# LN3's bias on GpSimd, the query transposes on TensorE: one change with three parts

## The chip, the cores and the metric

The kernel runs on one core of a Trainium2 chip. The metric is device time in microseconds (us) of one execution. TensorE (PE) multiplies matrices, VectorE (DVE), ScalarE (ACT) and GpSimd (POOL) work on vectors, and SyncE (SP) issues most DMAs. DMAs are also issued from ScalarE's and GpSimd's instruction streams, and stand in order with their other instructions.

## The reference

The input x has 2048 rows of 1024 bf16 values. What is computed:

```
h  = x + A(layernorm(x))                 # LN1, sliding dilated attention
out = h + B(layernorm(h))                # LN2, gated MLP that mixes over rows

A: q, k, v = x @ wqkv   (32 heads of 32); each row attends to 8 rows: itself and 2, 4, .. 14 back;
   softmax over these 8; @ wo
B: z = gelu(x @ w_in)   (2048 x 3584); z1 = first 1792 columns;
   z2 = layernorm(last 1792 columns)     # LN3
   g = w_sp @ z2 + b_sp[:, None]         # w_sp is 2048 x 2048
   (z1 * g) @ w_out
layernorm(x) = (x - mean) / sqrt(var + 1e-5), without weights
```

## The kernel before, in words

**Tiling.** Rows are worked on in 16 tiles of 128 (NT) and 4 chunks of 512 (NCH), with 4 tiles to a chunk (TPC). Weights sit in SBUF as bf16. A TensorE accumulator `acc` is 128 x 1024 fp32 in PSUM. Three of them turn round (`ps_acc`, bufs=3), and the tiles `tpa` into which TensorE transposes share this ring.

**Stage 1: the queries of chunk 0, in an order written out by hand.** For each tile of chunk 0, `ln(i)` takes statistics (lines 243 to 245), gets the reciprocal deviation (249, 250) and writes the normalised tile `xn` (255). The projection needs it transposed, in `xnT[0]`, eight blocks of 128 x 128 for a tile. `xpose` (line 267) transposes blocks on TensorE against the identity and lets ScalarE copy them out of PSUM (269), in two copies of four blocks each. `XPE` says how many of a tile's blocks go this way: 8, 8, 6 and 4. The other blocks, the last two of tile 2 and the last four of tile 3, are transposed by a DMA that is issued from ScalarE's queue (line 314). The loop over i runs the 16 matmuls of tile i (line 305). In their midst, after `XAT[i]` matmuls, stands the transposition of tile i+1. Then come `ln(i + 2)`, the copy of the queries to `qs0` on ScalarE (311), the DMA transpose of tile i+2's remaining blocks, and on SP a DMA transpose of `qs0` into `qT` for the attention (315). The load of the value weights, wv (316), is bound to come behind the last of these on SP. The key weights, wk, are loaded by line 237.

**Stage 2: from the keys of chunk 0 to the end of the first half of B, ordered by a planner.** `Order` is a list scheduler that runs while the program is built. Operations are added with an engine, an estimated duration, what they depend on, a priority and a latency. It starts from estimated clocks (TensorE 22.3, ScalarE 23.4, VectorE and GpSimd 18.0), and emits the operations in the order of their planned start. TensorE, ScalarE and VectorE keep that order. SP's and GpSimd's own order is chosen by the compiler's scheduler. The planner holds the key, value and query projections (`qkv`, line 398), the attention (`attention`: VectorE products L454, sums L457, logits on TensorE L506, weighted sums L609 and L611), the output projection with LN2 (`head`, matmuls L666), and the two parts of z (`b_z2`, L736; `b_z1`, L786). Chunk by chunk, TensorE does projections while VectorE does the attention.

**LN3.** In `b_z2`, ScalarE empties the accumulators into `u` with the gelu and sums up (743), then sums the squares (752). `batch_rstd` makes mean, variance and the power -1/2 from these sums: four small VectorE instructions (630 to 633), the power on GpSimd (635), and on VectorE the bias `nb` = -mean x rstd (639). For chunks 0 to 2 ScalarE then normalises the four tiles of `u` in place (765) with scale rstd and bias nb, and each is stored to `z2_d` (769). A tile of `u` can be written for the next chunk when its store is done. For chunk 3 VectorE normalises into `z2sb` (767), with mean and rstd.

**x of the later chunks.** `x_loads` (called behind chunk 1's transposes in the program's order) loads x tiles 8 and 9 one by one (`load_x`, line 215), and 10 to 15 as three pairs (line 823). ScalarE reads them for LN1's sums (362).

**Stage 3: the mixing over rows and the output projection** (L897, L903, L919, L921), with all of `z2sb` in SBUF. Its order is written out by hand. The change doesn't touch it.

Of the kernel before, what the change touches and what calls it, by code (L numbers as in the profile page):

```python
# [12 lines left out]
ALU = mybir.AluOpType  # L13
# [6 lines left out]
F, FH = 3584, 1792  # L20
P = 128
NT = S // P
CH = 512
NCH = S // CH
TPC = CH // P
# [7 lines left out]
NWARM = 11  # L33
XRB = 4
XAT = (12, 13, 10, 0)
XPE = (8, 8, 6, 4)
POOLLAT = 2.2
LMODE = (2, 2, 2, 2)
Z2ACT = (4, 4, 4, 0)
FILL = (0, 2, 2, 0)  # L40
ABDMA = ((0, 1), (0, 1), (0, 1), (0, 1))
SPLIT = 4
# [97 lines left out]
def kernel(  # L140
# [121 lines left out]
    def xpose(i, xn, *parts):  # L262
        for k0, k1 in parts:
            if i not in tps or i == 0:
                tps[i] = (ps_acc if i or k0 else ps_att).tile([P, KT, P], BF16, name="tpa" if i or k0 else "tp0", tag="acc" if i or k0 else "L")
            for a in range(k0, k1):
                T.transpose(tps[i][:, a, :], xn[:, a * P:(a + 1) * P], ident)
        for k0, k1 in parts:
            A.copy(xnT[0][:, k0:k1, i * P:(i + 1) * P], tps[i][:, k0:k1, :])
# [16 lines left out]
    with tc.manual_schedule(engines=manual):  # L286
        wsq = l1.tile([P, 1], FP32, name="wsq", tag="wsq")
        A.activation(wsq[:], eps_t[:], ACTF.Sqrt)
        xns = {}

        def ln(i):
            stats(i)
            rstd_of(i)
            xns[i] = norm(i)

        ln(0)
        for part in ((0, 2), (2, 5), (5, KT)):
            xpose(0, xns[0], part)
        ln(1)
        for i in range(TPC):  # L300
            acc = new_acc()
            for n, (nh, kt) in enumerate([(nh, kt) for kt in range(KT) for nh in range(2)]):
                if n == XAT[i] and i + 1 < TPC:
                    xpose(i + 1, xns[i + 1], (0, 4), *([(4, XPE[i + 1])] if XPE[i + 1] > 4 else []))
                T.matmul(acc[:, nh, :], xnT[0][:, kt, i * P:(i + 1) * P], wsb[0][:, kt, nh * CH:(nh + 1) * CH],  # L305
                         start=(kt == 0), stop=(kt == KT - 1))
            if i + 2 < TPC:
                ln(i + 2)
            if i == 0:
                qs0 = att.tile([P, TPC, DLO, P], BF16, name="qs0", tag="oT")  # L310
            A.copy(qs0[:, i], acc[:].rearrange("p a b -> p (a b)").rearrange("p (m dl) -> p dl m", dl=DLO))
            if i + 2 < TPC:
                j, kd = i + 2, XPE[i + 2]
                A.dma_start_transpose(xnT[0][:, kd:KT, j * P:(j + 1) * P], xns[j][:, kd * P:])
            qt_ = nc.sync.dma_start_transpose(att_in[0][0][:, :, i * P:(i + 1) * P], qs0[:, i])
    tc.add_manual_dep(dma(wsb[2][:], wq_view[:, :, 2 * D:3 * D]).ins, qt_.ins.name,
                      mybir.DependencyInfo(mybir.DependencyClass.NoSync, mybir.DependencyReason.DATA), reason="load wv behind the query transposes")
# [304 lines left out]
                G["avmid", c] = m_  # L622
        G["avdone", c], G["avq", c] = m_, oq

    def batch_rstd(key, sums, sqs, n, pfx, deps, prio, cols=slice(0, TPC), nb=True):
        def a1():
            if cols.start == 0:
                G[key] = {k: bp.tile([P, TPC], FP32, name=pfx + k, tag=pfx + k) for k in ("mean", "msq", "var", "rstd", "nb")}
            t = G[key]
            V.tensor_scalar(t["mean"][:, cols], sums(), 1.0 / n, None, op0=ALU.mult)  # L630
            V.tensor_tensor(t["msq"][:, cols], t["mean"][:, cols], t["mean"][:, cols], op=ALU.mult)
            V.scalar_tensor_tensor(t["var"][:, cols], sqs(), 1.0 / n, t["msq"][:, cols], op0=ALU.mult, op1=ALU.subtract)
            V.tensor_scalar(t["var"][:, cols], t["var"][:, cols], 0.0, EPS, op0=ALU.max, op1=ALU.add)
        s1 = add("DVE", 0.74, a1, deps, prio=prio)
        s2 = add("POOL", 1.05, lambda: nc.gpsimd.tensor_tensor(G[key]["rstd"][:, cols], G[key]["var"][:, cols], nhalf[:, cols], op=ALU.pow),
                 [s1], lat=POOLLAT)
        def a3():
            t = G[key]
            V.scalar_tensor_tensor(t["nb"][:, cols], t["mean"][:, cols], -1.0, t["rstd"][:, cols], op0=ALU.mult, op1=ALU.mult)
        return add("DVE", 0.16, a3, [s2], prio=prio) if nb else s2  # L640

    def head(c):
# [74 lines left out]
    def b_z2(c):  # L717
        st = {}
        sqd = []
        for il in range(TPC):  # L720
            evs = []
            for hf in range(2):
                wd = win_specs[hf][1]
                deps = [G["hnTs", c][il] if ("hnTs", c) in G else G["hnT", c], G["win", hf]]
                for half in range(4):
                    def mm(half=half, hf=hf, il=il, wd=wd):
                        if half == 0:
                            st["acc"] = G["accz", c, il, hf] = new_acc()
                            if il == 0 and hf == 0:
                                st["sums"] = bp.tile([P, TPC, 2], FP32, name="sums", tag="sums")  # L730
                                st["sqs"] = bp.tile([P, TPC], FP32, name="sqs", tag="sqs")
                        accf = G["accz", c, il, hf][:].rearrange("p a b -> p (a b)")
                        for kt in range(2 * half, 2 * half + 2):
                            for n0 in range(0, wd, CH):
                                n1 = min(n0 + CH, wd)
                                T.matmul(accf[:, n0:n1], hnTs[c][:, il, kt, :], wins[hf][:, kt, n0:n1],  # L736
                                         start=(kt == 0), stop=(kt == KT - 1))
                    m_ = add("PE", 0.8635 if hf == 0 else 0.65, mm, deps, prio=order(), take="acc" if half == 0 else None)
                    deps = [(m_, 0.0)]
                def ev(hf=hf, il=il, wd=wd):  # L740
                    if hf == 0:
                        st["u", il] = l1.tile([P, FH], BF16, name="u", tag="x4k", bufs=4)
                    A.activation(st["u", il][:, hf * 1024:hf * 1024 + wd], G["accz", c, il, hf][:].rearrange("p a b -> p (a b)")[:, 0:wd],
                                 ACTF.Gelu_apprx_tanh, accum_out=st["sums"][:, il, hf:hf + 1])
                evs.append(add("ACT", 1.02 if hf == 0 else 0.93, ev, [m_] + ([G["z2st", c - 1, il]] if c else []),
                               prio=2.0, free="acc", lat=0.25, table="gelu"))
            def sq(il=il):
                if c < NCH - 1:
                    junk = pools["bq"].tile([P, FH], BF16, name="junk", tag="junk", bufs=1)[:]
                else:  # L750
                    junk = z2sb[c * TPC + il][:]
                A.activation(junk, st["u", il][:], ACTF.Square, accum_out=st["sqs"][:, il:il + 1])
            sqd.append(add("ACT", 1.72, sq, evs + ([G["close"]] if c == NCH - 1 else [G["open"]]), prio=5.0, lat=0.25))
        def st_tot():
            st["stot"] = bp.tile([P, TPC], FP32, name="stot", tag="stot")
            V.tensor_tensor(st["stot"][:], st["sums"][:, :, 0], st["sums"][:, :, 1], op=ALU.add)
        s0 = add("DVE", 0.16, st_tot, sqd, prio=2.0)
        rs = batch_rstd(("l3", c), lambda: st["stot"][:], lambda: st["sqs"][:], FH, "l3", [s0], 2.0)
        for il in range(TPC):
            i = c * TPC + il  # L760
            def nrm(il=il, i=i):
                t = G["l3", c]
                z2 = st["u", il] if c < NCH - 1 else z2sb[i]
                if Z2ACT[c] > il:
                    A.activation(z2[:], st["u", il][:], ACTF.Identity, scale=t["rstd"][:, il:il + 1], bias=t["nb"][:, il:il + 1])
                else:
                    V.tensor_scalar(z2[:], st["u", il][:], t["mean"][:, il:il + 1], t["rstd"][:, il:il + 1], op0=ALU.subtract, op1=ALU.mult)
                if c < NCH - 1:
                    dma(z2_d[i * P:(i + 1) * P, :], z2[:])
            n_ = add("ACT", 1.75, nrm, [rs], prio=5.5) if Z2ACT[c] > il else add("DVE", 0.62, nrm, [rs], prio=2.5)  # L770
            G["z2st", c, il] = dma_op(3.0, lambda: None, [n_])
            G["z2n", c, il] = n_

# [41 lines left out]

    dma_op(8.0, load_wo, [G["ev", 0, 2, 1]])
    def x_loads():
        for i in range(2 * TPC, 2 * TPC + 2):
            load_x(i)
        for i in range(2 * TPC + 2, NT, 2):  # L820
            x_slot(i)
            x_slot(i + 1)
            dma(pairs[i // 2][:], x2d[i * P:(i + 2) * P, :].rearrange("(a p) d -> p a d", p=P))

    for c in range(1, NCH):
        ln1(c)
# [123 lines left out]
```

## Time and profile before

| | |
|---|---|
| time, median of 13 runs | 725.81 us (724.85 to 730.58) |
| profiled execution | 725.17 us, span 723.4 us |
| granted TensorE clock | 1.0 |
| TensorE busy | 712.3 us (98% of the span) |
| VectorE, ScalarE, GpSimd busy | 412.5, 235.7, 59.1 us |
| first matmul of the key projection (L398) | 24.81 us |
| last key, value or query projection | up to 193 us |
| first matmul of the mixing (L897) | 430.15 us |

The span runs from the first to the last event of the core's engines. The time of an execution also holds what lies around it. Positions are us from the start of the span. In a line of the timeline stand start, length, engine, line of the kernel, operation, what is written from what, the count, and in brackets how long the engine was idle before and what ended it. A "q" behind an engine's name is its instruction queue, as at a DMA's issue. In a line of the chain stand start, length and what ran. PEld is TensorE's loading of weights, which runs beside its matmuls.

### The profile page before, as it was taken

Reading aid. Unit: us, or ns where it says so; the run is one execution under the profiler, and the core shown is the slowest. Engines: PE = TensorE matmul, PEld = TensorE weight load, DVE = VectorE, ACT = ScalarE, POOL = GpSimd, SP = SyncE. Lnnn points to the kernel's source line nnn. Section 1 sums busy time; section 2 is a strip of 40 time slices with the busy share of each in tenths; the row PEclk is TensorE's granted clock in tenths of the full one; section 3 lists DMA queues with packets and bytes.
Section 4 is the critical chain, followed back from the end, with each engine's and each line's share of the span. In section 5 each row is a group of like instructions: output and inputs, shape, how many; then the busy total and the mean of one; then the engine's idle time right before and its main releaser. Section 6 shows DMA issues by size and latency. Waiting matters only on the chain.

```text
span 723.4 us, 8399 instructions
## 1 busy us (share of the span) xinstructions
PE 712.3 (98%) x3382; PEld 363.5 (50%) x3443; DVE 412.5 (57%) x445; ACT 235.7 (33%) x300; POOL 59.1 (8%) x75
## 2 busy tenths in 40 slices
PE   8899999999999999999999999999999999999998
PEld 3566665666644444445444444444444444444444
DVE  5698699989999899987970202222222222222222
ACT  4389452632346685766725520000000000000000
POOL 0011400012002202001114000000000000000000
PEclk9999999999999999999999999999999999999999
DMA  9995674567662951752338878453115311120002
GB/s 329 237 319 128 197 195 147 160 201 253 215 253 80 236 194 56 258 126 59 136 114 263 258 188 291 161 131 123 37 43 134 119 39 44 33 85 14 1 16 72
DMA packets 120790, 107.55 MB, mean 149 GB/s; under 512 B 73696, under 2 KB 99072, under 8 KB 120752
## 3 DMA queue, kind: packets, MB, share of 16 engines
q1 hardware_dynamic: 110592, 73.95, 34.8%
q0 software_dynamic: 7888, 31.43, 13.0%
q10 hardware_dynamic: 2272, 1.64, 1.0%
q8 instruction: 27, 0.44, 0.3%
q14 instruction: 11, 0.09, 0.0%
HBM read 55.09 MB, written 30.74 MB: 119 GB/s over the span
## 4 chain that ended last, share of the span: by engine, by line
PE 96%; DMA 2%; issue 1%; DVE 0%; SPq 0%; ACT 0%; ACTq 0%
PE acc L897 27%; PE acc L398 21%; PE acc L786 13%; PE acc L736 13%; PE acc L919 13%; PE acc L666 8%; DMA xp<-in_A_x_dram 1%; DMA xnT<-xn 1%; PE acc L305 1%; PE L L506 1%; SPq L233 0%; DVE bnst L243 0%; DVE bnst L244 0%; DVE xn L255 0%; DVE ot L921 0%
## 5 line engine op out<-in xcount | busy, mean ns | idle before, releaser
L897 PE MATMUL acc<-wspT,z2sb 128*128 128x512 bf16 x878 | 193.1, 379 | 0.9
L897 PEld LDWEIGHTS <-z2sb 128*128 128x128 bf16 x896 | 87.7, 98 | 105.7
L903 DVE TENSOR_TENSOR g<-acc,bB 128x1024 bf16<-128x1024 f32 x28 | 34.3, 1225 | 159.9 <-PE acc L897 135.1
L786 PE MATMUL acc<-hnT,win 128*128 128x512 bf16 x448 | 98.0, 379 | 0.0
L736 PE MATMUL acc<-win,hnT 128*128 128x512 bf16 (+1 forms) x501 | 97.3, 352 | 0.6
L736 PEld LDWEIGHTS <-hnT 128*128 128x128 bf16 x512 | 50.0, 98 | 47.3 <-issue 0.4
L919 PEld LDWEIGHTS <-zg 128*128 128x128 bf16 x462 | 45.2, 98 | 51.7
L786 PEld LDWEIGHTS <-win 128*128 128x128 bf16 x448 | 43.8, 98 | 52.6 <-issue 0.4
L454 DVE TENSOR_TENSOR prod<-qT,kT 128x4096 bf16<-128x4096 bf16 (+1 forms) x32 | 68.3, 2152 | 2.2 <-DMA kT<-qkv_d 1.6
L609 DVE TENSOR_TENSOR prod<-vT,AB 128x4096 bf16<-128x4096 bf16 (+1 forms) x32 | 64.3, 2023 | 0.7
L611 DVE TENSOR_TENSOR oT<-oT,prod 128x4096 bf16<-128x4096 bf16 (+1 forms) x32 | 64.5, 2018 | 0.1
L921 DVE TENSOR_TENSOR ot<-acc,hr 128x1024 bf16<-128x1024 f32 (+2 forms) x18 | 19.9, 1106 | 73.1 <-PE acc L919 64.2
L919 PE MATMUL acc<-wout_a,zg 128*128 128x512 bf16 (+1 forms) x260 | 58.0, 372 | 0.3
L398 PE MATMUL acc<-xnT,wk 128*128 128x512 bf16 x249 | 55.7, 379 | 0.5 <-issue 0.2
L666 PE MATMUL acc<-wo_sb,oT 128*128 128x512 bf16 x249 | 55.7, 379 | 0.4
L398 PE MATMUL acc<-xnT,wv 128*128 128x512 bf16 x252 | 55.7, 379 | 0.2
L409 ACT CAST stg<-acc 128x1024 bf16<-128x1024 f32 x36 | 36.4, 1010 | 57.3 <-PE acc L398 53.5
L398 PEld LDWEIGHTS <-wk 128*128 128x128 bf16 x256 | 36.9, 145 | 18.7 <-issue 0.4
L398 PEld LDWEIGHTS <-wv 128*128 128x128 bf16 x256 | 37.0, 145 | 18.2
L919 PE MATMUL acc<-wout_b,zg 128*128 128x512 bf16 (+1 forms) x193 | 43.8, 372 | 0.2
L398 PE MATMUL acc<-xnT,wq 128*128 128x512 bf16 x189 | 41.8, 379 | 0.3 <-issue 0.2
L792 ACT ACTIVATE z1s<-acc 128x1024 bf16<-128x1024 f32 x28 | 28.6, 1022 | 40.7 <-PE acc L786 30.6
(102 smaller groups left out, 507.0 us busy)
## 6 DMA issues: line engine op xcount, KB each, us to landing
qkv_d<-stg SPq DMA_DIRECT2D x36, 256.0 KB, 2.5
z_d<-z1s SPq DMA_DIRECT2D x28, 256.0 KB, 2.7
z1c<-z_d SPq DMA_DIRECT2D x28, 256.0 KB, 3.2
z_d<-u SPq DMA_DIRECT2D x12, 448.0 KB, 2.5
z2sb<-z_d POOLq DMA_DIRECT2D x12, 448.0 KB, 8.1
xr<-in_A_x_dram SPq DMA_DIRECT2D x16, 256.0 KB, 2.8
h_d<-hb SPq DMA_DIRECT2D x16, 256.0 KB, 2.1
win<-in_B_w_in_dram POOLq DMA_DIRECT2D x2, 2048.0 KB, 9.3
```

The source lines that it names most:

```text
L398: G["mmins", c, xi, dp] = T.matmul(G[key][:, j, :], wv[:, kt, dl, :], xnT[c][:, kt, :], start=(kt == 0), stop=(kt == KT - 1))
L409: A.copy(stg[:], G[key][:])
L454: V.tensor_tensor(qs[w]["prod"][:, d0:d1], qT[:, d0:d1], kT[:, d0:d1, o:o + CH], op=ALU.mult)
L609: V.tensor_tensor(dst[:, :, sq].rearrange("p d (q s) -> p d q s", q=nq), vv, abb, op=ALU.mult)
L611: V.tensor_tensor(oTs[c][:, :, sq], oTs[c][:, :, sq], pvs[w, q0][:, :, sq], op=ALU.add)
L666: T.matmul(st["acc", il][:, nh, :], oTs[c][:, dl, il * P:(il + 1) * P], wo_sb[:, dl, nh * CH:(nh + 1) * CH], start=(dl == 0), stop=(dl == ...
L736: T.matmul(accf[:, n0:n1], hnTs[c][:, il, kt, :], wins[hf][:, kt, n0:n1], start=(kt == 0), stop=(kt == KT - 1))
L786: T.matmul(G["accy", c, fp][:, j, :].rearrange("p (a b) -> p a b", a=TPC), wt[:, kt, f0 * P:(f0 + 1) * P], hnTs[c][:, :, kt, :], start=(kt ...
L792: A.activation(z1s[:], G["accy", c, fp][:], ACTF.Gelu_apprx_tanh)
L897: m_ = T.matmul(acc[:, j, :], z2sb[a][:, f * P:(f + 1) * P], wspT[:, a, :], start=(a == 0), stop=(a == NT - 1))
L903: V.tensor_tensor(g1[:], acc[:], bB[:, c * CH:(c + 1) * CH].unsqueeze(1).to_broadcast([P, 2, CH]), op=ALU.add)
L919: T.matmul(acc[:, m0 - n0:m1 - n0], zg[:, f, il * P:(il + 1) * P], wt[:, f0, m0:m1], start=(f == 0), stop=(f == NF - 1))
```

## The change: what it does

- `XPE` goes: TensorE transposes all eight blocks of tiles 2 and 3, too, and line 314's DMA is gone.
- `batch_rstd` gets `neg`. For LN3 of chunks 0 to 2, the mean is scaled by -1/n, and the bias is a GpSimd multiply of it with rstd, planned at 0.5 us directly behind the power. The power's latency of 2.2 us to ScalarE is planned behind the multiply. LN1, LN2 and LN3 of chunk 3 stay as they were.
- `Z2ACT` goes, with the same choice of engines as it had.
- `x_loads` loads tiles 8 to 13 one by one, and only 14 and 15 as a pair.

```diff
-XPE = (8, 8, 6, 4)
-Z2ACT = (4, 4, 4, 0)
...
                 if n == XAT[i] and i + 1 < TPC:
-                    xpose(i + 1, xns[i + 1], (0, 4), *([(4, XPE[i + 1])] if XPE[i + 1] > 4 else []))
+                    xpose(i + 1, xns[i + 1], (0, 4), (4, KT))
...
             A.copy(qs0[:, i], acc[:].rearrange("p a b -> p (a b)").rearrange("p (m dl) -> p dl m", dl=DLO))
-            if i + 2 < TPC:
-                j, kd = i + 2, XPE[i + 2]
-                A.dma_start_transpose(xnT[0][:, kd:KT, j * P:(j + 1) * P], xns[j][:, kd * P:])
             qt_ = nc.sync.dma_start_transpose(att_in[0][0][:, :, i * P:(i + 1) * P], qs0[:, i])
...
-    def batch_rstd(key, sums, sqs, n, pfx, deps, prio, cols=slice(0, TPC), nb=True):
+    def batch_rstd(key, sums, sqs, n, pfx, deps, prio, cols=slice(0, TPC), nb=True, neg=False):
...
-            V.tensor_scalar(t["mean"][:, cols], sums(), 1.0 / n, None, op0=ALU.mult)
+            V.tensor_scalar(t["mean"][:, cols], sums(), (-1.0 if neg else 1.0) / n, None, op0=ALU.mult)
...
         def a3():
             t = G[key]
-            V.scalar_tensor_tensor(t["nb"][:, cols], t["mean"][:, cols], -1.0, t["rstd"][:, cols], op0=ALU.mult, op1=ALU.mult)
+            if neg:
+                nc.gpsimd.tensor_tensor(t["nb"][:, cols], t["mean"][:, cols], t["rstd"][:, cols], op=ALU.mult)
+            else:
+                V.scalar_tensor_tensor(t["nb"][:, cols], t["mean"][:, cols], -1.0, t["rstd"][:, cols], op0=ALU.mult, op1=ALU.mult)
+        if neg:
+            return add("POOL", 0.5, a3, [(s2, 0.0)], lat=POOLLAT)
         return add("DVE", 0.16, a3, [s2], prio=prio) if nb else s2
...
-        rs = batch_rstd(("l3", c), lambda: st["stot"][:], lambda: st["sqs"][:], FH, "l3", [s0], 2.0)
+        rs = batch_rstd(("l3", c), lambda: st["stot"][:], lambda: st["sqs"][:], FH, "l3", [s0], 2.0, neg=c < NCH - 1)
...
-                if Z2ACT[c] > il:
+                if c < NCH - 1:
...
     def x_loads():
-        for i in range(2 * TPC, 2 * TPC + 2):
+        for i in range(2 * TPC, NT - 2):
             load_x(i)
-        for i in range(2 * TPC + 2, NT, 2):
-            x_slot(i)
-            x_slot(i + 1)
-            dma(pairs[i // 2][:], x2d[i * P:(i + 2) * P, :].rearrange("(a p) d -> p a d", p=P))
+        x_slot(NT - 2)
+        x_slot(NT - 1)
+        dma(pairs[NT // 2 - 1][:], x2d[(NT - 2) * P:NT * P, :].rearrange("(a p) d -> p a d", p=P))
```

More of the change, by code (lines that the diff above doesn't have):

```diff
@@ L769, in nrm @@
                     dma(z2_d[i * P:(i + 1) * P, :], z2[:])
-            n_ = add("ACT", 1.75, nrm, [rs], prio=5.5) if Z2ACT[c] > il else add("DVE", 0.62, nrm, [rs], prio=2.5)
+            n_ = add("ACT", 1.75, nrm, [rs], prio=5.5) if c < NCH - 1 else add("DVE", 0.62, nrm, [rs], prio=2.5)
             G["z2st", c, il] = dma_op(3.0, lambda: None, [n_])
```

## The prediction

> **What bounds the kernel now.** I read four views. The page first: its busy times, and its chain that ended last.
>
> ```profile
> PE 712.3 (98%) x3382; PEld 363.5 (50%) x3443; DVE 412.5 (57%) x445; ACT 235.7 (33%) x300; POOL 59.1 (8%) x75
> PE 96%; DMA 2%; issue 1%; DVE 0%; SPq 0%; ACT 0%; ACTq 0%
> ```
>
> TensorE is busy for 712.3 of 723.4 us and carries 96% of the chain, at full granted clock. So 11.1 us of it is all that anything but less TensorE work can win, and the place of those 11.1 us decides. The chain in order of time says where they lie:
>
> ```profile
> 13.22 0.55 DVE xn L255
> 13.77 0.03 DVE bnst L243
> 13.80 6.64 DMA xnT<-xn
> 20.44 0.05 issue
> 20.49 4.06 PE acc L305 x18
> 24.55 0.05 issue
> 24.60 0.38 PE acc L305
> 24.98 10.57 PE acc L398 x49
> ```
>
> From 20.49 to the last matmul, at 720.45, the chain is TensorE without a hole larger than 0.21 us ("issue"). Ahead of it stands a DMA transpose of 6.64 us, issued at 13.80. The timeline of the first 27 us shows what it holds up:
>
> ```profile
> 13.80 1.28 ACTq L314 DMA_TRANSPOSE xnT<-xn  x1
> 14.08 0.50 PE L267 MATMUL tpa<-csb,xn 128*128 128x128 bf16 x6
> 15.12 0.86 ACT L269 COPY xnT<-tpa 128x512 bf16<-128x512 bf16 x2 [1.24 <-DVE bnst L244]
> 15.77 2.33 PE L305 MATMUL acc<-wq,xnT 128*128 128x512 bf16 x10 [0.54 <-ACT xnT L269]
> 18.16 0.59 PE L305 MATMUL acc<-wq,xnT 128*128 128x512 bf16 x2
> 20.49 4.49 PE L305 MATMUL acc<-wq,xnT 128*128 128x512 bf16 x19 [1.73 <-DMA xnT<-xn]
> 20.92 4.87 SPq L315 DMA_TRANSPOSE qT<-qs  x3
> ```
>
> Two holes are seen on TensorE: 1.73 us until tile 2's last two blocks have landed, and 0.54 us until ScalarE has copied tile 2's first four out of PSUM. ScalarE was then issuing the DMA: from 13.80 for 1.28 us, so that its copy began at 15.12 although the transposes had ended at 14.08+0.50 = 14.58.
>
> **The change, part by part.** *Query stage.* Removed: two DMA transposes on ScalarE's queue (1.28 and 1.21 us of issue, 6.64 us to landing for the first) with their waits. Added: two transposes for tile 2 and four for tile 3 on TensorE. Their price comes from the rows of tile 1, where eight began at 9.92 and the next matmul at 10.41: 0.49 us for eight. Six cost 0.34 us here (14.08 to 14.42), four 0.23 (17.93 to 18.16).
>
> Up to 14.08 nothing changes. From there, with 0.216 us a matmul (ten from 15.77 to 17.93):
> - Tile 2's eight transposes: 14.08 to 14.57. Tile 1's i loop ends with three matmuls: 15.22.
> - ScalarE is free (its cast of tile 0 ended at 13.89). For tile 1 the copy began 0.65 us after the first transpose (10.57, 9.92); tile 2's next matmul came 0.65 us after its copy began (15.77, 15.12). So copy at 14.73, matmul at 15.38, not 15.77.
> - Ten matmuls to 17.54; eight transposes to 18.03; six matmuls to 19.33. Tile 3's xn was ready at 17.04 and no later now.
> - Tile 3's copies, two in 1.07 us as for tile 1, run from 18.19 to 19.26. Its 16 matmuls run from 19.33 to 22.79.
>
> The key projection (L398) then begins at 22.79 where it began at 24.81: **2.02 us less**. As a sum of differences: 1.88 us of idle in the stretch from 15.77 (9.04 us, less 32 x 0.216 and 0.23) goes, 0.39 is won at the copy, 0.23 to 0.26 is paid for the four added transposes of tile 3; tile 2's two cost 0.15 and lie in front of a wait that hides them. More than 0.16 us beyond that isn't to be had there: that is the hole left between 15.22 and 15.38.
>
> What the key projection needs is there: wk was issued at 5.92 and takes 11.5 us, so 17.4; its first accumulator needs tile 2's cast, 1.01 us from 19.55.
>
> *SP's queue.* In the waits of the DMA queue, the query transposes stand behind ScalarE's:
>
> ```profile
> SPq L315 <- DMA xnT<-xn: 8.7, 2, 8.3
> ```
>
> With those gone, the first three of L315 can go when their casts end (13.89, about 17 and 20.6) and not from 20.92 on. They meet wk: two of 3.4 us each could put wk at 24.2 at worst, 1.4 us too late, and at best change nothing, since the two removed transposes moved 192 KB at the same time. I take zero, the nearer row. The fourth follows the last cast, 24.0 instead of 26.02, and wv behind it is issued at about 25.35 (was 28.28). Wv takes 9.4 us: 34.75, for a first use at 38.41 - 2.02 = 36.39. VectorE's first product waited 4.42 us for qT (to 31.49); that wait shrinks, and what is late next is the key projection's own copy to kT (a 0.57 us wait at 39.87 now), which moves with TensorE. So VectorE moves by the same 2 us.
>
> *x loads.* Two single loads and three pairs become six singles and one pair: seven issues on SP for five; at 0.38 us for a single (L215's median) and 0.5 for a pair, some 0.5 us more. Tile 10 was loaded at 40.30 and landed 4.7 us later, for a use at 46.64; 1.6 us of cover, and ScalarE, which waits if it is gone, sits idle at many places: zero. If SP issues the four earlier, they come before wv (a rival below).
>
> *LN3.* For chunks 0 to 2 the sign goes into the mean (free: same instruction, and its square is the same), and one VectorE instruction of 0.16 us becomes one on GpSimd, behind the power there. The rows of this tile:
>
> ```profile
> L765 ACT ACTIVATE u<-u,l3nb,l3rstd x12: 1867/1872/1881, 255.5 to 358.9; 128x1792 bf16<-128x1792 bf16 x12
> L635 POOL TENSOR_TENSOR l3rstd<-l3var,nhalf x4: 1040/2255/2986, 251.4 to 409.5; 128x4 f32<-128x4 f32 x4
> L639 DVE SCALAR_TENSOR_TENSOR l3nb<-l3mean,l3rstd x4: 153/159/164, 253.1 to 410.5; 128x4 f32<-128x4 f32 x4
> ```
>
> No GpSimd multiply is in the trace. Its nearest row is the power on the same shape: 1.04 to 2.99 us; the lower bound is VectorE's 0.16. I take 1.04 when VectorE is quiet and up to 2.99 beside it. Removing the instruction from VectorE also removes a wait in its queue: in chunk 1 the power ended at 288.83 and nb ran only at 290.06, behind a 2.28 us product. So nb comes at 289.9 to 291.8 in place of 290.21. Behind it in GpSimd's queue stand DMA issues and LN2 powers that come 10 us later or more, and nothing new is waited for, since mean was there before the power. Who waits is ScalarE's L765. In chunk 0 that began 2.26 us after nb was ready. An accumulator written by b_z2(1) from 256.45 is asked for again three accumulators later, at 256.45 + 3.45 + 2.6 + 3.45 = 265.95, and ScalarE needs 1.2 us to empty it; it did so at 261.69: more than 3 us of cover. So this part is worth 0 to TensorE. It also changes the planner's sums (0.5 us on GpSimd for 0.16 on VectorE), so the order of ScalarE and VectorE behind 250 us can change.
>
> [...]
>
> **The sum.** Profiled execution: span 723.4, time 725.17, so 1.77 us outside the span. Span 723.4 - 2.02 = 721.4, time 723.15. The median of 13 is 725.81, 0.64 above the profiled one; the same 2.02 off it gives **723.8**.
>
> **Rivals.**
> 1. *Wv is late.* Four more x loads (1 MB) go out ahead of wv. For: two single x loads stand in front of the last L315 (25.84) already, and singles now number six. Against: SP is idle from about 21 to 24 and would have moved them by then. At wv's rate (2048 KB in 9.4 us) 1 MB is 4.7 us; less the cover of 36.39 - 34.75 = 1.64, TensorE waits 3.05: **726.8**.
> 2. *VectorE doesn't follow.* It is close behind TensorE: the head's weight load of chunk 1 waited 0.48 us for it and the matmul came 0.15 late (205.59 + 0.216 to 205.96):
>
> ```profile
> 205.96 13.50 PEld L666 LDWEIGHTS <-oT 128*128 128x128 bf16 x64 [0.48 <-DVE oT L611]
> ```
>
> One product of 2.29 us that the new order puts before the sum a head waits for costs TensorE about 2.3: **726.1**. Against: VectorE is set back to TensorE's time by the logits in each chunk (it waits 2.29, 2.37, 1.48 and 1.90 us for L506), and until 250 us the order isn't touched.
>
> 3. *Slower: the LN3 part costs more than the query stage wins.* The mechanism is the planner putting a chunk's four L765 (3.64 us a pair, 7.3 in a row) ahead of an emptying of an accumulator. TensorE has two more, so that emptying may be 2 x 3.45 - 1.02 = 5.8 us late; beyond that, 1.5 us of wait per chunk. Done in all three chunks it is 4.5 us: 723.8 + 4.5 = **728.3**. It decides once it passes 2.02 + 2.18 = 4.2 us. Against: in this trace they run in twos and ones with emptyings between, since these have the better priority.
>
> **Chances.** 0.3% of 725.81 is 2.18 us, about what a measurement of this kernel can tell from no change: bounds 723.63 and 727.99. The forecast's case gets 0.70, with its own range 723.1 to 724.6 (0.16 us that may still be won, run spread of some 0.4, small waits at VectorE's meetings). Its middle lies just inside the bound, so I give 0.32 to faster and 0.38 to the same. Rival 1 gets 0.09, rival 2 0.09 (both the same), rival 3 0.12. Together 0.32, 0.56, 0.12. The range 723.1 to 726.8 leaves out rival 3 and some ends of the first case.
>
> **What would show it.** Right: no L314, eight transposes in a row at 14.08 and near 17.5, no TensorE hole over 0.2 us from there, L398 from 22.8, the first L315 near 13.9, and the chain pure TensorE until about 718.4. In LN3, a GpSimd multiply of 1 to 3 us and no hole on TensorE between 250 and 365. Wrong: a hole ahead of wk's first matmul (near 22.8), of wv's (near 36.4), at an L666, or at L736 or L786 behind an L765.

## The result, and the profile after

The changed kernel takes 723.14 us (median of 14 runs, 722.71 to 727.15); the kernel before, in the 62 runs beside it, 725.39 us (724.47 to 730.58). The ratio is 0.9974, with a 95% interval of 0.9961 to 0.9986: 0.26% faster, a real gain, but inside the 0.3% that the prediction called "the same". The forecast was 723.8 us in a range of 723.1 to 726.8.

The profiled execution took 722.71 us with a span of 720.9 (before: 725.17 and 723.4), so its span is 2.5 us shorter. The page's busy times and its chain:

```profile
PE 713.3 (99%) x3388; PEld 364.3 (51%) x3449; DVE 412.5 (57%) x442; ACT 236.2 (33%) x301; POOL 63.4 (9%) x78
PE 98%; issue 0%; DVE 0%; DMA 0%; ACT 0%
```

TensorE is busy for 1.0 us *longer* than before, with six more instructions in the records (the six transposes), in a span that is 2.5 us shorter. VectorE has three instructions fewer (x442 for x445), GpSimd three more (x78 for x75): the LN3 part. TensorE's share of the chain is 98% for 96%, and DMA's, in which the transpose's 6.64 us were 0.9% of the span, is down from 2% to 0%.

The chain in order of time, over the stretch that the prediction worked out (start, length, what):

```profile
14.02 0.45 PE tpa L265 x8
14.46 0.66 PE acc L303 x3
15.13 0.02 issue
15.14 2.33 PE acc L303 x10
17.47 0.45 PE tpa L265 x8
17.92 3.02 PE acc L303 x14
20.94 0.05 issue
21.00 1.67 PE acc L303 x7
22.67 9.06 PE acc L393 x42
```

Where the chain of before left TensorE for 6.64 us of DMA at 13.80, it now stays on TensorE: eight transposes (L265, was L267), three matmuls (L303, was L305), ten, eight transposes, 21 matmuls, the key projection (L393, was L398). The timeline of the same stretch gives the starts and who released them:

```profile
13.67 8.23 SPq L310 DMA_TRANSPOSE qT<-qs  x3
13.86 0.61 PE L265 MATMUL tpa<-csb,xn 128*128 128x128 bf16 x8
14.50 1.07 ACT L267 COPY xnT<-tpa 128x512 bf16<-128x512 bf16 x2 [0.85 <-PE tpa L265]
15.14 1.84 PEld L303 LDWEIGHTS <-xnT 128*128 128x128 bf16 x10 [0.52 <-ACT xnT L267]
17.31 0.61 PE L265 MATMUL tpa<-csb,xn 128*128 128x128 bf16 x8
22.51 4.70 PE L393 MATMUL acc<-xnT,wk 128*128 128x512 bf16 x21
23.75 1.24 SPq L310 DMA_TRANSPOSE qT<-qs  x1
```

ScalarE's copy (L267) is now released by TensorE, 0.64 us after the first transpose, where it had started at 15.12 behind a DMA issue. From tile 2's first transpose to the key projection it is 22.51 - 13.86 = 8.65 us, where it was 24.81 - 14.08 = 10.73: 2.08 us less. SP's query transposes (L310, was L315) start at 13.67 instead of 20.92, and its 8.7 us wait for ScalarE's transposes has no line any more. What TensorE waited for, over the whole execution, with all its lines:

```profile
PE wps L221 <- DVE warm L218: 1.3, 1, 1.3
PE tp L265 <- DVE xn L253: 0.2, 1, 0.2
```

Both stand before the first real matmul. The remaining 0.4 us of the 2.5 are not in the edited stretch. Tile 2's transposes start 0.22 us earlier (13.86 for 14.08) because the first transpose of all does; in executions of kernels whose head up to there is unedited it lies anywhere from 6.28 to 6.60. And the second head's weight load, which had waited for VectorE, has no wait in its row:

```profile
203.29 13.70 PEld L666 LDWEIGHTS <-oT 128*128 128x128 bf16 x64
```

The head's first matmul starts 0.22 us behind the matmul ahead of it (203.28 to 203.50), where it started 0.37 us behind (205.59 to 205.96): 0.16 us less. In an execution of the kernel with the LN3 part alone, where nothing before 250 us was changed, it was 0.22 us as well (205.65 to 205.86); so those 0.16 us are scatter of the execution, not the edit. Behind it the 2.47 us of head start stay to the end (TensorE's chain ends at 717.98 for 720.45).

LN3's instructions, by tile (count, shortest/median/longest in ns, first and last start):

```profile
L765 ACT ACTIVATE u<-u,l3nb,l3rstd x12: 1864/1871/1882, 251.9 to 357.2; 128x1792 bf16<-128x1792 bf16 x12
L635 POOL TENSOR_TENSOR l3nb<-l3mean,l3rstd x3: 340/1283/1297, 250.6 to 349.0; 128x4 f32<-128x4 f32 x3
```

The multiply takes 0.34 us once and 1.28 and 1.30 us in the other two. The timeline of chunk 0, and after it that of chunk 2, shows when each of them ends:

```profile
249.57 2.28 DVE L604 TENSOR_TENSOR oT<-vT,AB 128x4096 bf16<-128x4096 bf16 x1
250.63 1.28 POOL L635 TENSOR_TENSOR l3nb<-l3mean,l3rstd 128x4 f32<-128x4 f32 x1
...
348.05 1.22 DVE L604 TENSOR_TENSOR prod<-vT,AB 128x2048 bf16<-128x2048 bf16 x1
348.99 0.34 POOL L635 TENSOR_TENSOR l3nb<-l3mean,l3rstd 128x4 f32<-128x4 f32 x1
```

In chunk 0 VectorE's product ends at 251.85 and the multiply at 251.91; in chunk 2 at 349.27 and 349.33. Chunk 1 is alike (286.45, 286.51). In all three chunks the multiply ends 0.06 us behind the VectorE product that ran when it began; that product still had 1.22, 1.24 and 0.28 us to run.

### The profile page after: what moved, and what is told of

It reads as the page before. It is cut to its first block, busy times and chain, and to the rows that moved or that the text cites. A ratio compares the mean times of both kernels' runs of the same rounds, so it can differ in the third digit from the quotient of the medians.

```text
span 720.9 us, 8410 instructions
## 1 busy us (share of the span) xinstructions
PE 713.3 (99%) x3388; PEld 364.3 (51%) x3449; DVE 412.5 (57%) x442; ACT 236.2 (33%) x301; POOL 63.4 (9%) x78
## 4 chain that ended last, share of the span: by engine, by line
PE 98%; issue 0%; DVE 0%; DMA 0%; ACT 0%
PE acc L896 27%; PE acc L393 21%; PE acc L786 13%; PE acc L736 13%; PE acc L918 13%; PE acc L666 8%; PE acc L303 2%; PE L L501 1%; DMA xp<-in_A_x_dram 0%; PE tpa L265 0%; DVE xn L253 0%; DVE bnst L241 0%; DVE bnst L242 0%; DVE ot L920 0%; PE tp L265 0%
## 5 line engine op out<-in xcount | busy, mean ns | idle before, releaser
L736 PE MATMUL acc<-win,hnT 128*128 128x512 bf16 (+1 forms) x501 | 97.3, 352 | 0.6
L736 PEld LDWEIGHTS <-hnT 128*128 128x128 bf16 x512 | 50.0, 98 | 47.3 <-issue 0.4
L393 PE MATMUL acc<-xnT,wk 128*128 128x512 bf16 x252 | 56.1, 379 | 0.2
L666 PE MATMUL acc<-wo_sb,oT 128*128 128x512 bf16 x249 | 55.7, 379 | 0.4
L393 PE MATMUL acc<-xnT,wv 128*128 128x512 bf16 x251 | 55.6, 379 | 0.3
L393 PEld LDWEIGHTS <-wk 128*128 128x128 bf16 x256 | 36.9, 145 | 18.6 <-issue 0.4
L393 PEld LDWEIGHTS <-wv 128*128 128x128 bf16 x256 | 37.0, 145 | 18.2
L393 PE MATMUL acc<-xnT,wq 128*128 128x512 bf16 x187 | 41.9, 379 | 0.3
```

The source lines that it names most:

```text
L393: G["mmins", c, xi, dp] = T.matmul(G[key][:, j, :], wv[:, kt, dl, :], xnT[c][:, kt, :], start=(kt == 0), stop=(kt == KT - 1))
L666: T.matmul(st["acc", il][:, nh, :], oTs[c][:, dl, il * P:(il + 1) * P], wo_sb[:, dl, nh * CH:(nh + 1) * CH], start=(dl == 0), stop=(dl == ...
```

## The experiments

The theory (A): the gain is made only in the query stage, as two holes of TensorE that go; LN3 and the x loads are worth nothing because other work covers them. Its rivals: the gain of the head is given back or made up elsewhere (VectorE, wv, LN3).

**The query stage alone.** All four tiles on TensorE; x loads and LN3 as before.

```
-XPE = (8, 8, 6, 4)
+XPE = (8, 8, 8, 8)
-            if i + 2 < TPC:
+            if i + 2 < TPC and XPE[i + 2] < KT:
                 ...  A.dma_start_transpose(...)
```

> The kernel before with all eight blocks of tiles 2 and 3 transposed on TensorE, and nothing else of the change. Theory A (the gain lies ahead of the key projection): the key projection begins 2.0 to 2.3 us earlier than the 24.81 us of before, and the time falls by 2.0 to 2.5 us from before. Theory B (the other two parts give a good share): the time falls by less than 1.5 us.

Measured: 723.2 us (11 runs), 0.9964 (0.9945 to 0.9984) of the kernel before. That is all of the change's gain. Profiled: transposes at 14.09, key projection at 22.74, again 8.65 us; here the start is as late as before, and these 2.08 us are all of the 2.1 that its span (721.3) is shorter.

```profile
14.09 0.61 PE L267 MATMUL tpa<-csb,xn 128*128 128x128 bf16 x8
22.74 4.48 PE L398 MATMUL acc<-xnT,wk 128*128 128x512 bf16 x20
```

**LN3 alone**, and **the x loads alone.**

```
+ def batch_rstd(..., neg=False)   # -1/n into mean; nb = gpsimd.tensor_tensor(mean, rstd)
+ rs = batch_rstd(("l3", c), ..., neg=c < NCH - 1)
```

> The kernel before with LN3's bias on GpSimd for chunks 0 to 2, and nothing else of the change. Theory A: within 0.3 us of before, no new hole on TensorE; the GpSimd multiply takes 0.3 to 1.3 us as in the profile after. Theory B: faster by 0.5 us or more, because VectorE's order is relieved.

```
-        for i in range(2 * TPC, 2 * TPC + 2):
+        for i in range(2 * TPC, NT - 2):
             load_x(i)
+        # one pair left: the last two tiles
```

> The kernel before with x tiles 8 to 13 loaded one by one, and nothing else of the change. Theory A: within 0.3 us of before; key projection at 24.8 us, wv not later. Theory C (the loads move SP's order, and with it the attention of chunk 1): the wait of TensorE at the head's first weight load near 206 us (0.16 us before, none after) goes, and 0.1 to 0.3 us are won.

Measured: 1.0003 (0.9994 to 1.0011) for LN3, 1.0005 (0.9997 to 1.0014) for the loads: no difference for either. In the LN3 kernel the multiply is as in the whole change, and no hole on TensorE follows it:

```profile
L640 POOL TENSOR_TENSOR l3nb<-l3mean,l3rstd x3: 341/1286/1297, 253.0 to 351.3; 128x4 f32<-128x4 f32 x3
```

So A's division of the gain stands: query stage all, the rest nothing.

**Which of the two DMA transposes cost it?** Both kernels are the kernel before with one tile changed: one keeps only tile 3's DMA (four blocks, issued from ScalarE), the other only tile 2's (two blocks).

```
 # only tile 2's blocks moved to TensorE      # only tile 3's
-XPE = (8, 8, 6, 4)                           -XPE = (8, 8, 6, 4)
+XPE = (8, 8, 8, 4)                           +XPE = (8, 8, 6, 8)
```

> The kernel before with only tile 2's last two blocks moved to TensorE; tile 3's last four are still transposed by the DMA on ScalarE's queue. Theory A (each DMA transpose costs its wait): the hole ahead of tile 2's copies goes (matmul near 15.4), a wait for tile 3's landing comes in place of tile 2's, since it is issued near 17 and took 3.8 us, behind SP's transpose that now runs first; key projection between 22.9 and 25.5 us, time 0.5 better to 1 us worse than before is possible, and not the full gain. Rival D (only tile 2's transpose cost anything): key projection near 22.6 us, all of the 2.1 us and 0.23 more.

> The kernel before with only tile 3's last four blocks moved to TensorE; tile 2's last two are still transposed by the DMA on ScalarE's queue. Theory A: both holes stay (0.5 us ahead of the copy, the wait for the landing 1 to 1.7 us), the four transposes add 0.23 us in front of a wait that hides them; key projection between 24.0 and 24.9 us; time within 0.8 us of before. Rival D: no gain at all, 24.8 us. Rival (tile 3's DMA is what delays the landing of tile 2's): the wait falls under 1 us, and the time by 1 us or more.

With tile 2's DMA in place, both holes are there, and the time of before with them: 724.93 us, 1.0 (0.9979 to 1.0021). Its timeline:

```profile
15.87 2.33 PE L305 MATMUL acc<-wq,xnT 128*128 128x512 bf16 x10 [0.55 <-ACT xnT L269]
20.27 4.49 PE L305 MATMUL acc<-wq,xnT 128*128 128x512 bf16 x20 [1.19 <-DMA xnT<-xn]
```

The copy is held up by 0.55 us, as before. The wait for the landing is shorter (1.19 for 1.73 us) only because TensorE does four more transposes ahead of it; the blocks land at much the same time (20.27 for 20.49).

With only tile 3's DMA in place, the query stage has no hole at all:

```profile
13.90 0.61 PE L267 MATMUL tpa<-csb,xn 128*128 128x128 bf16 x8
16.70 1.32 ACTq L314 DMA_TRANSPOSE xnT<-xn  x1
17.58 4.91 PE L305 MATMUL acc<-wq,xnT 128*128 128x512 bf16 x22
22.33 4.91 PE L398 MATMUL acc<-xnT,wk 128*128 128x512 bf16 x22
```

From tile 2's transposes (13.90) to the key projection (22.33) it takes 8.43 us, 0.22 *less* than with everything on TensorE, which is the price of the four transposes. The rival won this stage, and A's forecast of a remaining wait was wrong. The DMA, issued at 16.70, lands 3.5 us later, at 20.2, before its first use near 20.4. Tile 2's DMA in the other kernel was issued 2.80 us earlier, at 13.90, and landed no earlier, at 20.23. So part of the 6.64 us that the prediction read as one transfer is waiting. The load of wk was issued at 5.83 and 5.66 us in the two; at the 11.2 to 11.5 us that it took in the profiles after and before, it was on its way until an estimated 17 us. Whether that is what the DMA waits for, and whether moving wk would have closed the holes too, was not tested. But the time of this kernel is 723.72 us, 0.9983 (0.9967 to 0.9999), not lower than the whole change. Its profiled execution was one of the two longest of its twelve (727.27 us, span 725.5), and has waits on TensorE that the changed kernel's has not:

```profile
PE acc L666 <- DVE oT L611: 2.0, 2, 1.3
PE acc L736 <- ACT z1s L792: 1.7, 1, 1.7
```

The first is the wait of the prediction's second rival, a head's weights that VectorE delivers late. In this kernel the query transposes on SP begin at 20.33 again, behind the DMA from ScalarE, and VectorE's first product at 29.55, 7.2 us after the key projection starts; in the changed kernel it is 5.4. That VectorE's later start causes the waits is suggested by this, not shown; and since they stand in one of the longest executions, how much of them is in the median stays open.

**The same DMA from SP's queue.** Does the price lie in ScalarE's queue, which the issue held for 1.28 us before?

```
-A.dma_start_transpose(xnT[0][:, kd:KT, ...], xns[j][:, kd * P:])
+nc.sync.dma_start_transpose(xnT[0][:, kd:KT, ...], xns[j][:, kd * P:])   # XPE as before
```

> The kernel before with its two DMA transposes of x issued by SP in place of ScalarE. It parts the two holes: ScalarE's issue time is gone, the wait for the landing stays. Theory A: the matmul behind tile 2's copies begins 0.65 us after a copy that is no longer held up, near 15.4 (15.77 before); the wait for the landing stays, perhaps shorter, since SP needs no wait between two queues. The time falls by 0.3 to 1.5 us. Rival: the landing is bound by the DMA engines alone, and the key projection starts at 24.8 as before, no gain.

Slower: 729.41 us, 1.0066 (1.0049 to 1.0082). The copy starts on time (14.48), as expected, but the landing is bound by the DMA: tile 2's blocks are there at 20.29, so TensorE only waits longer, 2.18 us in place of 1.73.

```profile
20.29 6.18 PE L305 MATMUL acc<-wq,xnT 128*128 128x512 bf16 x19 [2.18 <-DMA xnT<-xn]
41.91 3.46 PE L398 MATMUL acc<-xnT,wv 128*128 128x512 bf16 x15 [1.63 <-DMA wv<-in_A_wqkv_dram]
```

Then two things came that no theory here had. The 19 matmuls take 6.18 us where 19 took 4.49 before: the granted clock fell, by the table of windows (length, busy time and count of PE, PEld, DVE, ACT, POOL, then PEclk, DMA share, GB/s):

```profile
22.00:24.00 2.00, 2.00 (x6) 0.66 (x5) 1.74 (x5) 0.74 (x1) 0.09 (x1) 0.50 0.99 94
```

Until 24.36 the matmuls come every 0.43 us (by their weight loads), and from the landing to the key projection (26.30) it takes 6.01 us in place of 4.32. And in SP's queue the transposes of the next stage slid ahead of the last query transpose, so that wv went out at 32.94 instead of 28.28 and TensorE waited 1.63 us for it. Two more waits, 2.2 us at L666 for VectorE and 1.6 us at L736 for ScalarE, are those of the kernel above; this profiled execution too is a long one (732.64 us). The two holes of before are thus not independent: the copy's delay alone is hidden behind the landing, and only taking the DMA away wins both.

**How much cover has LN3?** The multiply repeated, 4 and 12 times, in the changed kernel.

```
-                nc.gpsimd.tensor_tensor(t["nb"][:, cols], t["mean"][:, cols], t["rstd"][:, cols], op=ALU.mult)
+                for _ in range(4):   # or 12
+                    nc.gpsimd.tensor_tensor(t["nb"][:, cols], t["mean"][:, cols], t["rstd"][:, cols], op=ALU.mult)
```

> The changed kernel with the GpSimd multiply of LN3 done four times in a row, planner's costs unchanged. The run with twelve showed in chunk 0 a normalisation 27.0 us late and a hole of 23.6 us on TensorE, so 3.4 us of cover, and in chunk 2 one 11 us late and a hole of 5.2, so about 6. Three more multiplies of 0.3 to 1.3 us (up to 2.2 each beside VectorE) make the bias 1 to 7 us later. If the cover is right: holes only beyond 3.4 us in chunk 0, so the time is within 0.4 us of the changed kernel's 723.1 if they take 1.1 us each, and up to 4 us more if they take 2.2 each. Rival (no cover, every microsecond of GpSimd counts): 3 to 12 us more.

> The changed kernel with the GpSimd multiply of LN3 done twelve times in a row, with the planner's costs unchanged; each takes 0.34 to 1.3 us, so the bias comes 4 to 14 us later in each of chunks 0 to 2. Theory A (the LN3 part costs nothing because ScalarE's normalisation has 3 to 5 us of cover): now the cover is gone, holes appear on TensorE in b_z1 or b_z2 behind L765, 1 to 8 us a chunk, 5 to 20 us in all. Rival: ScalarE never holds TensorE up, time as after.

Four: 730.07 us, 1.0059 (1.0031 to 1.0087) of the kernel before. Twelve: 755.7 us, 1.0414 (1.0384 to 1.0445). The holes in chunk 0, by the timelines, first of four and then of twelve:

```profile
265.36 11.02 PE L737 MATMUL acc<-win,hnT 128*128 128x512 bf16 x46 [5.46 <-ACT z1s L793]
```

```profile
283.53 16.70 PE L737 MATMUL acc<-win,hnT 128*128 128x512 bf16 x71 [23.58 <-ACT z1s L793]
```

With twelve, the multiply by tile:

```profile
L636 POOL TENSOR_TENSOR l3nb<-l3mean,l3rstd x36: 198/1057/2249, 252.7 to 387.8; 128x4 f32<-128x4 f32 x36
```

With four, the first L766 (ScalarE's LN3, L765 before) came 8.8 us later than in the changed kernel (260.75 for 251.95) and TensorE lost 5.46; with twelve, 26.97 later and 23.58 lost. The differences give a cover of 3.3 and 3.4 us, and TensorE is made to wait by the emptying of an accumulator, the mechanism that the prediction named. Four cost more than expected, because beside VectorE's 2.28 us products the four took 8.02 us together and because the clock stayed down behind the hole:

```profile
264.00:266.00 2.00, 0.64 (x2) 0.25 (x2) 2.00 (x2) 2.00 (x3) 0.00 (x0) 0.50 0.69 278
266.00:268.00 2.00, 2.00 (x6) 0.71 (x5) 1.97 (x2) 2.00 (x4) 0.00 (x0) 0.50 0.63 224
270.00:272.00 2.00, 2.00 (x13) 1.12 (x12) 1.97 (x2) 1.97 (x3) 0.00 (x0) 1.00 0.56 229
```

Six matmuls in 2 us at 0.50, thirteen at 1.00.

Twelve in a row also show how the multiply's time went with VectorE's work. In chunk 0, beside twelve VectorE products of 2.28 us without a gap, they took 26.14 us, 2.18 each; in chunk 2, mostly beside products of 1.22 us, 12.35 us, 1.03 each; in chunk 1 all twelve took 6.27 us and made no hole; VectorE was idle for 1.5 us in their midst. Five of them passed there in 1.31 us, and the last of the twelve ended at 317.35, 0.09 us behind the instruction with which VectorE went on (L673, 316.03 to 317.26). So in chunk 0 one multiply got through per product, and the shortest of the 36 took 0.20 us (198 ns).

**Rival 1, brought about:** x tiles 8 to 11 bound ahead of wv on SP.

```
+    for k in range(2 * TPC, 3 * TPC):
+        x_slot(k)
+        tc.add_manual_dep(dma(xts[k], ...).ins, qt_.ins.name, ...)   # ahead of the load of wv
```

> The changed kernel with x tiles 8 to 11 (1 MB) loaded directly ahead of wv on SP, bound behind the last query transpose. It makes the rival of the late wv happen. By that rival's price (wv's rate, 2048 KB in 9.4 us, so 4.7 us later, and 1.6 us of cover): TensorE waits about 3 us ahead of the value projection, and the time is 3 us above the changed kernel's 723.1. If SP's issue alone is late (four issues, 1.6 us) and the transfers share the engines: 0 to 1 us.

724.32 us, 0.9983 (0.9971 to 0.9996): 1.2 us above the changed kernel's median. TensorE's wait:

```profile
38.22 1.95 PE L397 MATMUL acc<-xnT,wv 128*128 128x512 bf16 x8 [1.80 <-DMA wv<-in_A_wqkv_dram]
```

The rival's mechanism exists; its price was set at 3.05 us and is 1.80. Wv landed 4.1 us later than in the changed kernel (2.0 by its issue, 2.1 by a landing that took 11.1 us for 9.0), not 4.7, and the cover was 2.0 us, not 1.64.

**Towards a better kernel.** The changed kernel's first transpose needs xn and an identity, a 32 KB load that GpSimd issues at 1.22 us; in some of the profiles above the identity is the later of the two, landing 5.0 us behind its issue. Three tries to start earlier: the load on ScalarE's queue; the same with tile 3's four blocks by DMA as well; the identity made in SBUF by GpSimd.

```
 # 1: -dma_w(csb[:, 0:128], ...)   +A.dma_start(csb[:, 0:128], ...)   behind the load of x tile 1
 # 2: 1, and   xpose(..., (0, 4), *([(4, KT)] if i + 1 < 3 else []))
 #             if i == 1: A.dma_start_transpose(xnT[0][:, 4:KT, 3*P:4*P], xns[3][:, 4*P:])
 # 3: nc.gpsimd.memset(csb[:, 0:128], 1.0); nc.gpsimd.affine_select(csb[:, 0:128], ..., compare_op=ALU.is_equal, fill=0.0)
```

> The changed kernel with the identity for the transposes loaded from ScalarE's queue behind the second x tile, in place of GpSimd's. In the profiles so far the first transpose waited for it (0.2 to 0.9 us, csb) or came right at its landing. If it is what holds the start up: the first transpose 0.3 to 0.5 us earlier, near 5.9 us, and 0.2 to 0.35 us of that left at the key projection, since tile 2's xn is ready only 0.3 us ahead of its use; time 722.8. Rival: x, wq or the statistics hold it up as well, no change.

> The changed kernel with the identity from ScalarE's queue, and with tile 3's last four blocks transposed by a DMA on ScalarE's queue again. In the run that moved only tile 2's blocks, that DMA landed in time, and the key projection began 0.22 us earlier, counted from tile 2's transposes, than with all blocks on TensorE; but SP's query transposes started at 20.3 in place of 13.7, and VectorE began 1.6 to 1.9 us later. If the head alone counts: 722.6. If VectorE's later start costs TensorE its waits at the heads: 723.2 to 724.

> The changed kernel with the identity for the transposes made by GpSimd in SBUF (ones, then a select on the diagonal) in place of loaded; GpSimd has nothing else to do before 23 us. Two runs that loaded it from ScalarE's queue had it 1.2 to 1.7 us later than GpSimd's load, and the time got worse by as much or more. If its landing is what holds the first transpose: it now begins when the first 256 columns of xn are there, near 5.8 us (6.3 in the profile after), and the key projection near 22.2; tile 2's xn, ready 0.3 us ahead of its use, lets no more than 0.3 us through: 722.8. Rival: nothing won, 723.1, since xn and x set the pace.

The first missed: issued at 1.67, behind two x loads on ScalarE's queue, the 32 KB landed later, 6.2 us behind the issue, not earlier. (The profile names VectorE as releaser, but xn's three parts were done at 6.53; the second kernel's row names the load.) TensorE sat idle for 1.86 us, and from 9.98 to 12.96 us its weight loads came every 0.43 us, half the pace of 0.216, through most of its first 12 matmuls:

```profile
7.99 0.27 PE L265 MATMUL tp<-csb,xn 128*128 128x128 bf16 x2 [1.86 <-DVE mv L243]
...
8.72 4.45 PE L303 MATMUL acc<-wq,xnT 128*128 128x512 bf16 x12
```

The key projection came at 25.78; 725.51 us, 0.9995 (0.9967 to 1.0023). The second has the same fault at a smaller size (first transpose at 7.52), and its profiled execution has a granted clock of 1.0, with the same 12 matmuls in 2.76 us:

```profile
7.52 0.27 PE L265 MATMUL tp<-csb,xn 128*128 128x128 bf16 x2 [1.39 <-DMA csb<-qt_consts]
...
8.26 2.76 PE L303 MATMUL acc<-wq,xnT 128*128 128x512 bf16 x12
```

Its query stage again takes 8.43 us (14.97 to 23.40); 725.42 us, 1.0004 (0.9974 to 1.0034). Its key projection is only 0.9 us later than the changed kernel's, its time 2.3 longer; a head's weight load waits for VectorE here too (0.6 us). The clock is part of the rest: in seven of the twelve executions its mean was below 1 (0.995 or 0.998; 725.23 to 733.48 us), in the other five 1.0 (723.79 to 724.93). The first try is alike, six and six (725.74 to 733.81, and 724.14 to 725.29).

The third did what was expected of its start: the first transpose at 6.01 (6.30), the key projection at 22.20 (22.51). But in the compiled order of SP's queue, four x loads and a transpose of the next stage now stood ahead of the last query transpose, so wv was issued at 27.85 in place of 25.04:

```profile
36.94 1.30 PE L394 MATMUL acc<-xnT,wv 128*128 128x512 bf16 x5 [0.77 <-DMA wv<-in_A_wqkv_dram]
```

0.77 us lost for 0.31 won: 723.61 us, 0.9976 (0.9963 to 0.9989). That is rival 1, by an order that nobody wrote. No version tried is shown to be faster than the changed kernel.

## Why the prediction was right, point by point

- *Where the kernel is bound.* Right. TensorE's stretch from 14 to 25 us was the whole gain: the query stage alone gave 0.9964, the two other parts alone gave nothing.
- *The sum of 2.02 us.* Right: 2.08 in the profile of the changed kernel, and 2.08 with the query stage alone. Its sub-steps, as differences: the copy 0.65 us behind the first transpose (measured 0.64), the next matmul 1.30 behind it (1.28), tile 3's transposes 3.46 behind tile 2's (3.45). In its sum of differences the 1.88 works out to 1.90 (9.04 - 6.91 - 0.23); the 2.02 comes from the positions and doesn't change.
- *What the sum did not see.* It took the two holes as they stood and gave tile 3's transposes as part of the price of closing them. The runs showed that tile 2's DMA alone made both holes; tile 3's lands in time, and moving it to TensorE costs 0.22 us. The time is no better without that move, though.
- *SP's queue.* Right within 0.3 us: the first query transpose at 13.67 (near 13.9), the fourth at 23.75 (24.0), wv at 25.04 (25.35). The two that meet wk did not make it late: no wait at L393. Wv's first weights are loaded at 36.1 and it lands at 34.0, so the cover is 2.0 us (1.64).
- *VectorE follows.* Right. Its wait for qT shrank from 4.4 to 1.1 us, and what it waits for instead is the key projection's copy to kT (1.5 us, was 0.6).
- *x loads.* Right, zero by themselves. Two of the six singles went out ahead of wv (at 22.00), as before, and four behind it (at 36.61), so rival 1 did not come.
- *LN3, the multiply's duration.* The bounds were VectorE's 0.16 and the power's 2.99 us, with 1.04 taken as the quiet value and 2.99 as the busy one. It is 0.34 to 1.30, and in the repeated multiplies 0.20 to 2.25: the sort of range was right, the reason given for it too loose. The row of the power, another instruction, did not tell the multiply's duration: in the changed kernel it was what VectorE's running product had left, 0.28 to 1.24 us, plus 0.06 us.
- *LN3, the cover.* "More than 3 us" is 3.3 to 3.4 by the repetitions. The sum did not need the duration, only that it is below the cover, and that is why the misfit cost nothing. Rival 3 did not come (in its price, 2 x 3.45 - 1.02 is 5.9, not 5.8, so it was set 0.3 us too high).
- *The price of a hole.* Rivals 1 and 2 priced a wait at its length. The profiled executions have no further loss of clock behind waits of 1.73 and 1.80 us (granted clock 1.00); behind 2.18 us (the DMA on SP's queue) the matmuls lost another 1.69, so a hole like that one cost more than its length.
- *The median.* 723.14 against 723.8, at the low end of the range. The query stage's 2.02 was taken off a median of 725.81; the median over 62 runs is 725.39, and that accounts for 0.42 of the 0.66. On which side of the bound it fell was as close as the forecast had it: 2.25 us by the medians is 0.31%, the ratio says 0.26%, and its interval (0.14% to 0.39%) holds the bound of 0.3%.

## What to carry to other kernels

When a matmul engine that is busy 98% of the time waits for a small DMA, doing the same work on the busy engine can be the cheaper way: tile 2's two transposes at 0.06 us closed 2.3 us of holes, and the other four closed none. Look at which of two transfers makes the hole, and at the queue it blocks on its way (here ScalarE's copy, for which TensorE waited 0.54 us, and SP's query transposes, which waited 8.7), before pricing them together. A step hidden behind a cover needs no exact duration, only the cover's size: repeat the step until it shows, and then also check the order in which the compiler leaves the queues, which moved wv by 2.8 us for an edit elsewhere.

## What the runs showed of the hardware that was not expected

TensorE's granted clock fell behind some short holes. In the profiled executions it stayed at 1.00 behind idle times of 1.39 us (the second try for the identity), 1.73 (the kernel before) and 1.80 (the kernel of rival 1). Behind 1.86 us (the first try), 2.18 (the DMA on SP's queue), 5.46 (four multiplies), and 5.18 and 23.58 (twelve) a matmul came every 0.43 us instead of 0.216. By the weight loads that lasted for 3.0 us of work in the first try (9.98 to 12.96), 3.3 with the DMA on SP's queue (21.05 to 24.36), 3.7 behind four multiplies (265.36 to 269.08) and 5.9 behind the longest hole (283.53 to 289.45). A hole of 2.18 us so cost 2.18 + 1.69 = 3.87.

By the tables of windows the clock was still 1.00 from 18 to 20.2 us with the DMA on SP's queue, where the hole ended at 20.29, then 0.67 to 22, 0.50 to 24 and 0.94 to 26. With four multiplies it was 1.00 in 260:262, 0.54 in 262:264, while TensorE was still idle, 0.50 to 268, 0.75 in 268:270 and 1.00 behind that. What decides when it falls and when it rises was not shown.

The 32 KB load of the identity had no fixed time to land: 4.9 to 5.2 us after its issue by GpSimd, 5.7 and 6.2 us behind two x loads on ScalarE's queue. Making the same identity in SBUF took GpSimd 0.20 and 0.29 us.

The GpSimd multiply, 0.20 us at its shortest, lasted until the end of the VectorE product it met: 0.34 to 1.30 us in the changed kernel, each ending 0.06 us behind the product, and 2.18 us a piece in a row beside 2.28 us products. While VectorE was idle for 1.5 us, five of them passed in 1.31 us. What holds the multiply up was not tested.
